# Theta's weights queued behind later softmax groups, and the rounding of x in theta's units on ScalarE for every batch

## The chip, the cores and the metric

The kernel runs on one core of a Trainium2 chip. TensorE (PE) multiplies matrices, its weight loads stand as PEld in the profile; VectorE (DVE), ScalarE (ACT) and GpSimd (POOL) work element by element; SyncE (SP) issues most DMAs. The metric is the device time of one execution in microseconds (us), as the median of several runs.

## The reference

Three parts follow one another on q, k, v of 4 batches, 8 heads, 576 positions and 64 values a head (model width 512). Attention keeps a window of 32 positions (first four heads) or 32 positions at a stride of 4 (the others):

```python
scores = np.where(masks, scale * q @ k.T, -1e9)
attn = exp(scores - max); attn = attn / (sum + 1e-9)
x = attn @ v                       # heads side by side: 576 x 512
theta = x @ w_theta
y = w_tok_r @ (x * cos(theta)) + w_tok_i @ (x * sin(theta))
u = x + y
x2 = u + np.maximum(u @ w_ch, 0)
h = np.maximum(x2 @ w_in, 0); u, v = h[:, :512], h[:, 512:]
v_n = (v - mean(v)) / sqrt(var(v) + 1e-6)
out = (u * (w_spatial @ v_n + b_spatial[:, None])) @ w_out
```

## The kernel before

Every product with a weight is made of three matmuls of float32r halves: high by high, high by low, low by high. A "rounding" makes the high half of a value (a copy to float32r), a subtraction the low half. Weights that come as 64 bit words are put together from bits first: `bits64` (L116 to L136) loads them (L123), scales them on POOL or ACT (L132, L130) and joins the bits with three DVE instructions (L133 to L135); `split_weight` (L138) then rounds (L108 on ACT, L110 on DVE, L112 on POOL) and subtracts (L146).

Attention of a batch has 12 groups of scores (`groups`, four pairs of heads by three groups). For each group PE makes the scores (L245 with the mask by matmul in batch 0, L252), DVE the maximum (L259 in batch 0; L263 and L264 elsewhere), ACT three exponentials with their sums (L267), DVE the sum's reciprocal (L268, L269), POOL the product `sm` (L270). Two groups later PE transposes it (L280) and DVE or ACT copies it (L282, `pT`); four groups later PE multiplies it with v (L294, L298), and ACT copies the result into x (L301, or L306, L307, L309, L310). Transposes and these results share three PSUM buffers (`ps_t`).

`th_unit` (L339) makes theta for 128 positions of a batch b: it rounds x in units of turns (`xh`, two buffers: ACT L352 for batch 0, DVE L354 for the others), takes the low half on DVE (`xl`, L355), does 12 matmuls (L360), removes whole turns (ACT L368, DVE L369), takes two sines on ACT (L377, L378), multiplies with x transposed (DVE L381; L388, L389 for the last rows) and splits the results zh and zl (L110, L112, L332). There are five units in batches 0 and 1, four in batch 2, one for the last 64 rows of batches 2 and 3 together (`xs`), and four in batch 3: 14 of the 19 are not of batch 0. `tm_run` (L415) multiplies with w_tok (L431, L438), `ch_run` (L446) with w_ch (L457). Batch b's token product runs among the attention of batch b+1.

Some weights are prepared in between and stored to DRAM for later: each part goes through one of two shared buffers `parts` (rounding, subtraction, then a store by SP, L159 for weights, L464 for x2 of a batch). Of w_spatial (`w_sp`, loaded into `stage` at L142) seven of eight parts are made among the attention of batch 3, the roundings on ACT (L108), the subtractions on POOL (L146). A part must wait for the store of the part two before it.

The order on each engine comes from a scheduler that works over the whole program with durations of its own (L841, `schedule_with_timeline_sim`), within the program's dependences. `behind` (L504) adds an edge without a semaphore: what is issued inside stands behind the given instruction on that instruction's engine. Theta's eight weight parts (`w_theta_job`, k and half c) are so tied to the exponentials, the reciprocal and the product of a group of the first softmax; nothing on SP is among these, so their DMAs are not tied. The three lines that set it:

```python
TH_FROM, TH_RATE = 6, 6
            if m == TH_FROM + TH_RATE * i // 10:
                behind(softmax[m], lambda: w_theta_job(i // 2, i % 2))
```

Parts 0 to 7 so stand behind groups 6, 6, 7, 7, 8, 9, 9 and 10 (counted from 0).

Of the kernel before, what the change touches and what calls it, by code (L numbers as in the profile page):

```python
# [16 lines left out]
ALU = mybir.AluOpType  # L17
# [19 lines left out]
INV2PI = float(np.float32(1.0 / (2.0 * math.pi)))  # L37
# [2 lines left out]


LAG_T, LAG_V = 2, 4
TH_FROM, TH_RATE = 6, 6
TOK_RATE = 2.25
ATT_RATE, ATT_RATE_PAIR = 2.0, 3.0
TAIL_RATE = 1.0
# [17 lines left out]
def tile_block(ctx: ExitStack, tc: tile.TileContext, qT, kT, vw, eye_in, mask_in, eye_b_in, w_theta, w_tok, w_ch, w_in, w_sp, w_sph, b_sp, w_out, out):  # L64
    nc = tc.nc
    V, A, G, PE, SY = nc.vector, nc.scalar, nc.gpsimd, nc.tensor, nc.sync

    def f32(ap):
        return ap.bitcast(F32)
# [260 lines left out]
    def split(dst_h, dst_l, src, eh="a", el="g"):  # L330
        copy(dst_h, src, eh)
        return (G if el == "g" else V).tensor_tensor(dst_l, src, f32(dst_h), op=ALU.subtract)  # L332

    def ztile(k, bufs=1):
        h = pz.tile([P, DM], F32R, tag=f"zh{k}", name=f"zh{k}", bufs=bufs)
        l = pz.tile([P, DM], F32R, tag=f"zl{k}", name=f"zl{k}", bufs=bufs)
        return h, l

    def th_unit(b, t, pair=False):  # L339


        n = P if pair or t < 4 else HALF
        if pair:
            src = xs[b]
            V.tensor_copy(src[:, :, HALF:], x[b + 1][:, :, 4 * P:])
        else:
            src = x[b][:, :, P * t:P * t + n]
        h = pth.tile([P, 4, P], F32R, tag="xh", name="xh", bufs=2)[:, :, :n]
        l = pth.tile([P, 4, P], F32R, tag="xl", name="xl", bufs=2)[:, :, :n]

        if b == 0:
            A.mul(h, src, INV2PI)  # L352
        else:
            V.tensor_scalar(h, src, INV2PI, None, op0=ALU.mult)  # L354
        V.scalar_tensor_tensor(l, src, INV2PI, f32(h), op0=ALU.mult, op1=ALU.subtract)  # L355
        ps = ps_mm.tile([P, 512], F32, tag="mm", name="ps_th")[:n]
        i = 0
        for k in range(4):
            for lh, rh in ((h, wth_h), (l, wth_h), (h, wth_l)):
                PE.matmul(ps, lh[:, k, :], rh[:, k, :], start=(i == 0), stop=(i == 11))  # L360
                i += 1
        if b == 0 and t in (0, 1):
            if not t:
                spare.append(p1.tile([P, 4, DM], F32, tag="uh", name="spare"))
            ta, tb = (spare[0][:, 2 * t + i, :] for i in range(2))
        else:
            ta, tb = (pth.tile([P, DM], F32, tag=g, name=g, bufs=2)[:n] for g in ("ta", "tb"))
        A.activation(ta, ps, AF.Identity, bias=magic[:n, 0:1])  # L368
        V.scalar_tensor_tensor(ta, ta, MAGIC, ps, op0=ALU.subtract, op1=ALU.subtract)  # L369
        xn = ps_t.tile([P, 512], F32, tag="pt", name="ps_xn")[:n]  # L370
        for k in range(4):
            turned[b, t] = PE.transpose(xn[:, P * k:P * (k + 1)], src[:, k, :], ident)
        if b == 0:
            A.activation(tb, ta, AF.Abs)
        else:
            V.tensor_scalar(tb.bitcast(U32), ta.bitcast(U32), 0x7FFFFFFF, None, op0=ALU.bitwise_and)
        A.activation(ta, ta, AF.Sin, scale=-TURN)  # L377
        ia = A.activation(tb, tb, AF.Sin, scale=-TURN, bias=half_pi[:n, 0:1])  # L378
        if t < 4:
            for k, tt in ((t, tb), (4 + t, ta)):  # L380
                iv = V.tensor_tensor(tt, xn, tt, op=ALU.mult)  # L381
                zh[b, k], zl[b, k] = ztile(k)
                zlast[b] = ia, iv, split(zh[b, k], zl[b, k], tt, Z_HI[k // 4], "g")
        else:
            for i in range(2 if pair else 1):
                r_ = slice(HALF * i, HALF * (i + 1))
                zz = pth.tile([P, DM], F32, tag=("ta", "tb")[i], name="zz", bufs=2)
                V.tensor_tensor(zz[:HALF], xn[r_], tb[r_], op=ALU.mult)  # L388
                V.tensor_tensor(zz[HALF:], xn[r_], ta[r_], op=ALU.mult)  # L389
                zh[b + i, 8], zl[b + i, 8] = ztile(8, 2)  # L390
                split(zh[b + i, 8], zl[b + i, 8], zz, "a", "g")
# [9 lines left out]
    def th_shared(b):  # L401
        th_unit(b, 4, True)
        yield

    def th_run(b, ts):
        for t in ts:
            th_unit(b, t)
            yield
# [436 lines left out]
```

## Time and profile before

| | us |
|---|---|
| median of 3 runs (554.42 to 559.04) | 554.44 |
| the profiled execution, its device time | 554.9 |
| its span, first to last instruction | 553.1 |
| PE busy | 531.0 |
| DVE busy | 320.3 |
| POOL busy | 262.9 |
| ACT busy | 244.2 |

Times in the trace are counted from the span's start. PE is the engine with the most work. A row of a timeline gives start, duration, engine, line, operation, and in brackets the idle time of the engine in front of it with what ended that. Idle time of another engine costs only what PE then waits.

### The profile page before, as it was taken

Reading aid. Unit: us, or ns where it says so; the run is one execution under the profiler, and the core shown is the slowest. Engines: PE = TensorE matmul, PEld = TensorE weight load, DVE = VectorE, ACT = ScalarE, POOL = GpSimd, SP = SyncE. Lnnn points to the kernel's source line nnn. Section 1 sums busy time; section 2 is a strip of 40 time slices with the busy share of each in tenths; the row PEclk is TensorE's granted clock in tenths of the full one; section 3 lists DMA queues with packets and bytes.
Section 4 is the critical chain, followed back from the end, with each engine's and each line's share of the span. In section 5 each row is a group of like instructions: output and inputs, shape, how many; then the busy total and the mean of one; then the engine's idle time right before and its main releaser. Section 6 shows DMA issues by size and latency. Waiting matters only on the chain.

```text
span 553.1 us, 11234 instructions
## 1 busy us (share of the span) xinstructions
PE 531.0 (96%) x4148; PEld 474.5 (86%) x4148; DVE 320.3 (58%) x835; ACT 244.2 (44%) x717; POOL 262.9 (48%) x333
## 2 busy tenths in 40 slices
PE   5997999999999999988999999999999999999997
PEld 3665888989889989877889999899899889988996
DVE  2698998898787487632694139862702148253020
ACT  3869765635656254663452114542322233233221
POOL 3494994645984359641188336363202204322040
PEclk9999999999999999998999999999999999999999
DMA  8925766660588353770005978848015110002002
GB/s 203 300 93 156 191 180 189 182 198 35 162 235 232 95 175 120 230 228 25 1 1 155 370 250 286 265 131 289 20 58 172 58 38 1 1 1 77 0 1 96
DMA packets 50223, 76.07 MB, mean 138 GB/s; under 512 B 4084, under 2 KB 30968, under 8 KB 50168
## 3 DMA queue, kind: packets, MB, share of 16 engines
q1 hardware_dynamic: 49944, 75.17, 44.3%
q8 instruction: 33, 0.54, 0.4%
q10 hardware_dynamic: 224, 0.18, 0.1%
q14 instruction: 22, 0.18, 0.1%
HBM read 52.53 MB, written 22.81 MB: 136 GB/s over the span
## 4 chain that ended last, share of the span: by engine, by line
PE 52%; DMA 3%; POOL 1%; ACT 1%; issue 1%; DVE 1%; SPq 0%; ACTq 0%; POOLq 0%; DVEq 0%
PE ps_sp L719 9%; PE ps_hu L700 9%; PE ps_o L748 9%; PE ps_hv L655 9%; PE ps_y L438 7%; PE ps_r L457 4%; PE ps_th L360 1%; DMA wsp_d<-parts 1%; DMA win_d<-parts 1%; PE ps_sp L722 1%; PE ps_sp L721 1%; POOL zl L332 0%; POOL parts L146 0%; ACT parts L108 0%; DVE ta L381 0%
## 5 line engine op out<-in xcount | busy, mean ns | idle before, releaser
L438 PE MATMUL ps_y<-wtok_h,zh 128*128 128x288 f32 x270 | 82.1, 308 | 0.7 <-DVE sm L263 0.4
L438 PE MATMUL ps_y<-wtok_h,zl 128*128 128x288 f32 x270 | 81.0, 301 | 0.4 <-POOL zl L332 0.4
L438 PE MATMUL ps_y<-wtok_l,zh 128*128 128x288 f32 x270 | 79.8, 299 | 0.0
L332 POOL TENSOR_TENSOR gl<-hu,gh 128x288 fp32r<-128x288 f32 x32 | 26.0, 813 | 71.4 <-ACT gh L108 71.4
L438 PEld LDWEIGHTS ps_y<-wtok_h,zh 128*128 128x128 f32 x270 | 50.7, 189 | 3.2 <-DVE sm L263 0.9
L438 PEld LDWEIGHTS ps_y<-wtok_h,zl 128*128 128x128 f32 x270 | 51.2, 189 | 1.7 <-POOL zl L332 0.8
L723 DVE TENSOR_TENSOR hu<-ps_sp,hu 128x288 f32<-128x288 f32 x32 | 14.6, 456 | 63.5 <-PE ps_sp L722 63.5
L438 PEld LDWEIGHTS ps_y<-wtok_l,zh 128*128 128x128 f32 x270 | 50.7, 189 | 0.6
L332 POOL TENSOR_TENSOR vl<-hv,vh 128x512 fp32r<-128x512 f32 x16 | 20.9, 1308 | 58.1 <-ACT vh L108 53.1
L270 POOL TENSOR_TENSOR sm<-sm,l 128x288 f32<-128x288 f32 x48 | 32.0, 672 | 27.6 <-DVE l L269 14.7
L267 ACT ACTIVATE sm<-sm,m 128x96 f32<-128x96 f32 x108 | 39.2, 364 | 12.8 <-DVE m L264 6.7
L332 POOL TENSOR_TENSOR ul<-x,uh 128x288 fp32r<-128x288 f32 x32 | 26.7, 841 | 26.4 <-ACT uh L108 26.1
L719 PE MATMUL ps_sp<-wsp_h,vh 128*128 128x288 f32 x128 | 37.8, 295 | 0.0
L457 PE MATMUL ps_r<-uh,wch_h 128*128 128x288 f32 x128 | 37.6, 300 | 0.2 <-DVE x L441 0.2
L719 PE MATMUL ps_sp<-wsp_l,vh 128*128 128x288 f32 x128 | 37.8, 295 | 0.0
L719 PE MATMUL ps_sp<-wsp_h,vl 128*128 128x288 f32 x128 | 37.8, 295 | 0.0
L700 PE MATMUL ps_hu<-x2h,win_h 128*128 128x288 f32 x128 | 37.7, 294 | 0.0
L700 PE MATMUL ps_hu<-x2h,win_l 128*128 128x288 f32 x128 | 37.7, 294 | 0.0
L700 PE MATMUL ps_hu<-x2l,win_h 128*128 128x288 f32 x128 | 37.7, 294 | 0.0
L457 PE MATMUL ps_r<-uh,wch_l 128*128 128x288 f32 x128 | 37.5, 296 | 0.0
L441 DVE TENSOR_TENSOR x<-ps_y,x 128x288 f32<-128x288 f32 x40 | 17.6, 448 | 33.9 <-PE ps_y L438 33.8
L457 PE MATMUL ps_r<-ul,wch_h 128*128 128x288 f32 x128 | 36.7, 295 | 0.0
(182 smaller groups left out, 1577.7 us busy)
## 6 DMA issues: line engine op xcount, KB each, us to landing
x2d<-parts SPq DMA_DIRECT2D x32, 288.0 KB, 2.7
vt<-vw SPq DMA_DIRECT2D x16, 432.0 KB, 4.6
w<-w_tok SPq DMA_DIRECT2D x18, 288.0 KB, 4.7
x2h<-x2d SPq DMA_DIRECT2D x8, 576.0 KB, 7.8
x2l<-x2d SPq DMA_DIRECT2D x8, 576.0 KB, 8.3
kt<-kT SPq DMA_DIRECT2D x15, 304.0 KB, 4.2
w<-w_in SPq DMA_DIRECT2D x16, 256.0 KB, 3.3
win_d<-parts SPq DMA_DIRECT2D x16, 256.0 KB, 2.5
```

Of the source, the lines that this page charges most:

```text
L267: ia = A.activation(sm[:, t, :], src[:, t, :], AF.Exp, bias=m_[:, t:t + 1], scale=scale, accum_out=l[:, t:t + 1])
L270: ig = G.tensor_tensor(sm, sm, l.unsqueeze(2).to_broadcast([P, 3, KW]), op=ALU.mult)
L332: return (G if el == "g" else V).tensor_tensor(dst_l, src, f32(dst_h), op=ALU.subtract)
L360: PE.matmul(ps, lh[:, k, :], rh[:, k, :], start=(i == 0), stop=(i == 11))
L438: PE.matmul(ps[:, :CH], lh[b, k][:, P * d:P * (d + 1)], rh[:, k, cs], start=(n == 0), stop=(n == 3 * len(ks) - 1))
L441: V.tensor_tensor(xv, ps[:, :CH], xv, op=ALU.add)
L457: PE.matmul(ps[:, :CH], lh[:, k, P * e:P * (e + 1)], rh[:, k, cs], start=(n == 0), stop=(n == 11))
L655: PE.matmul(ps, lh[:, k, ts_], rh[:, k, DM:], start=(n == 0), stop=(n == 11))
L700: PE.matmul(ps[:, :CH], lh[:, k, fs], rh[:, k, cs], start=(n == 0), stop=(n == 11))
L719: PE.matmul(ps[:, :CH], lh[b, k][:, fs], rh[:, k, cs], start=(n == 0), stop=False)
L723: V.tensor_tensor(t[:, f, cs], ps[:, :CH], t[:, f, cs], op=ALU.mult)
L748: PE.matmul(ps, lh[:, k, ts_], rh[:, k, cs], start=(n == 0), stop=(n == 11))
```

## The change

Theta's weight parts are tied to later groups: `TH_FROM + TH_RATE * i // 10` is now 8, 8, 9, 9, 10, 10, 11, 11. And `xh` is rounded on ACT in all 19 units. The new file has three lines fewer, so its line numbers from L355 on are lower by 3 (and ACT's rounding is L351 there).

```diff
-TH_FROM, TH_RATE = 6, 6
+TH_FROM, TH_RATE = 8, 5
...
-        if b == 0:
-            A.mul(h, src, INV2PI)
-        else:
-            V.tensor_scalar(h, src, INV2PI, None, op0=ALU.mult)
+        A.mul(h, src, INV2PI)
         V.scalar_tensor_tensor(l, src, INV2PI, f32(h), op0=ALU.mult, op1=ALU.subtract)
```

The first place is DVE in the first softmax, where theta's first weight part begins (`c64` and `w64g` are its bits, `m`, `l` and `pT` belong to attention). Before:

```order
L259 TENSOR_REDUCE m_468<-s_458 128x3
L133 TENSOR_SCALAR c64_96<-wth64_333 128x256
L282 COPY pT_311<-pt_307 96x384
L134 SCALAR_TENSOR_TENSOR c64_96<-w64g_335,c64_96 128x256
L268 TENSOR_SCALAR l_426<-l_426 128x3
L259 TENSOR_REDUCE m_512<-s_502 128x3
L135 SCALAR_TENSOR_TENSOR w64g_335<-w64g_335,c64_96 128x256
L269 RECIPROCAL l_426<-l_426 128x3
L133 TENSOR_SCALAR c64_96<-wth64_342 128x256
L259 TENSOR_REDUCE m_562<-s_552 128x3
```

And now:

```order
L259 TENSOR_REDUCE m_441<-s_431 128x3
L282 COPY pT_311<-pt_307 96x384
L268 TENSOR_SCALAR l_390<-l_390 128x3
L269 RECIPROCAL l_390<-l_390 128x3
L133 TENSOR_SCALAR c64_96<-wth64_399 128x256
L259 TENSOR_REDUCE m_485<-s_475 128x3
L259 TENSOR_REDUCE m_544<-s_534 128x3
L268 TENSOR_SCALAR l_442<-l_442 128x3
L134 SCALAR_TENSOR_TENSOR c64_96<-w64g_401,c64_96 128x256
L269 RECIPROCAL l_442<-l_442 128x3
```

The copy, a sum and its reciprocal now stand in front of the first weight part, and the maxima of the last two groups (m_512 and m_562 before, m_485 and m_544 now) close behind its first instruction.

The second place is SP in the attention of batch 3, with the parts of w_spatial (parts_3630, 3698, 3713, 3719, 3725, 3731 and 3992 are the first to the seventh, `vt` is v of a pair of heads). Before:

```order
L159 DMA wsp_d_75<-parts_3630 128x2x288
L218 DMA vt_3399<-vw 96x1152
L142 DMA stage_3726<-w_sp 128x288
L159 DMA wsp_d_75<-parts_3698 128x2x288
L142 DMA stage_3732<-w_sp 128x288
L159 DMA wsp_d_75<-parts_3713 128x2x288
L142 DMA stage_3993<-w_sp 128x288
L159 DMA wsp_d_75<-parts_3719 128x2x288
L218 DMA vt_3536<-vw 96x1152
L142 DMA stage_4224<-w_sp 128x288
L159 DMA wsp_d_75<-parts_3725 128x2x288
```

And now:

```order
L159 DMA wsp_d_75<-parts_3630 128x2x288
L142 DMA stage_3726<-w_sp 128x288
L159 DMA wsp_d_75<-parts_3698 128x2x288
L218 DMA vt_3399<-vw 96x1152
L142 DMA stage_3732<-w_sp 128x288
L159 DMA wsp_d_75<-parts_3713 128x2x288
L142 DMA stage_3993<-w_sp 128x288
L159 DMA wsp_d_75<-parts_3719 128x2x288
L142 DMA stage_4224<-w_sp 128x288
L159 DMA wsp_d_75<-parts_3725 128x2x288
L589 DMA stage_4533<-w_sph 128x288
L218 DMA vt_3536<-vw 96x1152
```

Each of the two loads of v has moved behind a store of parts: vt_3399 behind that of the second part, vt_3536 behind that of the fifth.

The third place is ACT in the same stretch, from the rounding of the fourth part on (sm_3545, sm_3569 and sm_3608 are the last three groups of batch 3). Before:

```order
L108 CAST parts_3719<-stage_3720 128x288
L301 COPY x3_3154<-ps_x_3443 128x384
L108 CAST parts_3725<-stage_3726 128x288
L282 COPY pT_3461<-pt_3457 96x384
L301 COPY x3_3154<-ps_x_3518 128x192
L282 COPY pT_3530<-pt_3526 96x384
L108 CAST parts_3731<-stage_3732 128x288
L267 ACTIVATE sm_3545,l_3547<-sm_3545,m_3546 128x96 x3
L267 ACTIVATE sm_3569,l_3571<-sm_3569,m_3570 128x96 x3
L108 CAST parts_3992<-stage_3993 128x288
```

And now:

```order
L108 CAST parts_3719<-stage_3720 128x288
L282 COPY pT_3423<-pt_3419 96x384
L267 ACTIVATE sm_3470,l_3472<-sm_3470,m_3471 128x96 x3
L108 CAST parts_3725<-stage_3726 128x288
L301 COPY x3_3154<-ps_x_3443 128x384
L282 COPY pT_3461<-pt_3457 96x384
L108 CAST parts_3731<-stage_3732 128x288
L301 COPY x3_3154<-ps_x_3518 128x192
L282 COPY pT_3530<-pt_3526 96x384
L108 CAST parts_3992<-stage_3993 128x288
L267 ACTIVATE sm_3545,l_3547<-sm_3545,m_3546 128x96 x3
L267 ACTIVATE sm_3569,l_3571<-sm_3569,m_3570 128x96 x3
```

The seventh part's rounding has moved in front of the exponentials of sm_3545 and sm_3569, and each of the others stands one group earlier.

## Rows read from the trace of the kernel before

**Rows 1.** The page: busy time, share of the span, instructions of PE.

```profile
PE 531.0 (96%) x4148; PEld 474.5 (86%) x4148; DVE 320.3 (58%) x835; ACT 244.2 (44%) x717; POOL 262.9 (48%) x333
```

**Rows 2.** One stretch of 10 us: length, busy PE, PEld, DVE, ACT, POOL, then clock, DMA, GB/s.

```profile
50.00:60.00 10.00, 8.16 (x56) 6.39 (x55) 9.97 (x20) 8.22 (x17) 8.77 (x9) 1.00 0.94 246
```

**Rows 3.** Timeline of DVE, first softmax and theta of batch 0.

```profile
23.90 0.43 DVE L133 TENSOR_SCALAR c<-wth 128x256 uint32<-128x256 uint32 x1 [1.68 <-DMA wth<-w_theta]
24.24 0.54 DVE L282 COPY pT<-pt 96x384 f32<-96x384 f32 x1
...
25.34 0.44 DVE L259 TENSOR_REDUCE m<-s 128x3 f32<-128x288 f32 x1
...
47.95 0.68 DVE L388 TENSOR_TENSOR zz<-ps_xn,tb 64x512 f32<-64x512 f32 x1 [1.26 <-ACT tb L378]
```

**Rows 4.** Timeline of POOL, the same stretch.

```profile
23.96 0.42 POOL L132 TENSOR_SCALAR w64g<-wth 128x256 f32<-128x256 f32 x1 [2.66 <-DMA wth<-w_theta]
24.34 0.67 POOL L270 TENSOR_TENSOR sm<-sm,l 128x288 f32<-128x288 f32 x1
...
39.41 0.74 POOL L146 TENSOR_TENSOR wth_l<-w64g,wth_h 128x256 fp32r<-128x256 f32 x1
```

**Rows 5.** Timeline of PE: a wait in the first attention, theta's first and last shared matmuls.

```profile
27.78 0.87 PE L280 MATMUL pt<-ident,sm 128*96 128x128 f32 x6 [1.07 <-ACT x L301]
...
35.47 0.47 PE L360 MATMUL ps_th<-wth_h,xh 128*64 128x512 f32 x1
...
40.90 0.62 PE L360 MATMUL ps_th<-wth_l,xh 128*64 128x512 f32 x2
```

**Rows 6.** The lines of the rounding of x: instructions, duration min/median/max in ns.

```profile
L352 ACT ACTIVATE xh<-x x5: 420/617/627, 34.8 to 50.2; 128x512 fp32r<-128x512 f32 x4, 128x256 fp32r<-128x256 f32 x1
...
L354 DVE TENSOR_SCALAR xh<-x x13: 414/428/958, 110.7 to 275.5; 128x512 fp32r<-128x512 f32 x12, 128x256 fp32r<-128x256 f32 x1
```

**Rows 7.** Timeline of ACT, batch 2's theta and batch 3's attention.

```profile
194.01 0.43 ACT L108 CAST parts<-x 128x288 fp32r<-128x288 f32 x1 [2.93 <-DMA win_d<-parts]
...
245.25 0.43 ACT L108 CAST parts<-stage 128x288 fp32r<-128x288 f32 x1 [1.59 <-DMA wsp_d<-parts]
245.59 0.37 ACT L267 ACTIVATE sm<-sm,m 128x96 f32<-128x96 f32 x1
...
249.58 0.43 ACT L108 CAST parts<-stage 128x288 fp32r<-128x288 f32 x1 [1.73 <-issue]
...
250.54 0.36 ACT L267 ACTIVATE sm<-sm,m 128x96 f32<-128x96 f32 x1
```

**Rows 8.** Timeline of SP's queue, batch 3's attention.

```profile
242.43 0.38 SPq L159 DMA_DIRECT2D wsp_d<-parts  x1
242.90 0.42 SPq L218 DMA_DIRECT2D vt<-vw  x1
...
244.04 0.38 SPq L159 DMA_DIRECT2D wsp_d<-parts  x1
```

**Rows 9.** Timeline of POOL, batch 3's attention, its last product.

```profile
252.28 0.67 POOL L270 TENSOR_TENSOR sm<-sm,l 128x288 f32<-128x288 f32 x1 [0.77 <-DVE l L269]
```

**Rows 10.** Timeline of PE, its three longest waits in batch 3's attention.

```profile
242.06 0.50 PE L280 MATMUL pt<-ident,sm 128*96 128x128 f32 x3 [1.69 <-ACT x L301]
...
251.57 0.53 PE L280 MATMUL pt<-ident,sm 128*96 128x128 f32 x3 [1.83 <-POOL sm L270]
253.00 0.53 PE L280 MATMUL pt<-ident,sm 128*96 128x128 f32 x3 [0.90 <-POOL sm L270]
```

**Rows 11.** The same view by single microseconds, end of batch 3's attention.

```profile
250.00:251.00 1.00, 0.00 (x0) 0.00 (x0) 0.07 (x1) 1.00 (x6) 0.92 (x2) 1.00 0.02 6
...
252.00:253.00 1.00, 0.10 (x1) 0.00 (x0) 0.46 (x2) 0.79 (x4) 0.67 (x1) 1.00 0.69 242
...
254.00:255.00 1.00, 1.00 (x16) 0.88 (x13) 0.00 (x0) 0.47 (x2) 0.00 (x0) 0.54 0.00 0
...
257.00:258.00 1.00, 1.00 (x15) 0.88 (x12) 0.00 (x0) 0.36 (x2) 0.00 (x0) 0.76 0.00 0
```

## The prediction

> **What bounds the kernel now.** I read the page first, for the engine with the most work. PE is busy 531.0 of a span of 553.1 us [rows 1], so all its waits together are 22.1 us, and nothing that this change touches makes or removes a matmul. What can be won or lost is therefore a part of those waits, and one thing besides, the granted clock. I then listed PE's waits in order of time. They lie in four places: the start of the program, which the change leaves alone, the first attention with theta of batch 0, from 24 to 54 us, the middle of the attention of batch 3, from 240 to 254 us, and half a microsecond here and there. From 75 to 215 us PE is full. The reader is to see in the timeline of PE which instruction ended each wait: an x copy of ACT in the first attention (1.07 us) [rows 5], and then in batch 3 another x copy (1.69 us) and twice the product `sm` of POOL (1.83 and 0.90 us) [rows 10]. Last I looked at the clock by single microseconds: behind that second pair of waits, in which PE was busy 0.00 of one microsecond and 0.10 of another, the granted clock stood at 0.54 in the microsecond from 254 and was back only within that from 257, where it was 0.76 [rows 11]. That is about 3.4 us at the lower of the two levels (1.2 instead of 2.4 GHz), in which PE did the work of half that time, so 1.7 us were lost there.
>
> **Part A, theta's weights in the first softmax.** Before, DVE comes to theta's first weight part at 23.90 − 1.68 = 22.22 us and stands 1.68 us until its DMA has landed, at 23.90 [rows 3]; POOL stands 2.66 us for the same DMA [rows 4]. Attention's work is queued behind on both: on DVE the copy `pT`, the sum's step L268 and the maximum of the next group, on POOL a product `sm`. With the edges moved to groups 8 to 11 the copy, the sum and the reciprocal pass in front of the weight part, while DVE would have idled, and `sm` of groups 8 and 9 passes on POOL. Between the first weight instruction (starting 23.90) and the maximum at 25.34 there stood three others from 24.24 on; they are gone from there, so the maximum starts about 24.24, that is 25.34 − 24.24 = 1.10 us earlier [rows 3]. The last groups follow from it, and theta's first matmul, at 35.47, can start by as much earlier [rows 5].
>
> What is late next? First, the weights themselves: eight parts now stand behind later groups, and the last low half was made on POOL at 39.41 + 0.74 = 40.15, while the last matmuls of the first unit's chain that need it started at 40.90 [rows 4, 5]. The margin of 0.75 us stays if the weights gain as much as the attention, which they do in my replay of the order, since they are the same instructions without the waits between them. Second, DVE. From 50 to 60 us it is busy 9.97 of 10 us [rows 2], with w_tok's bits, the multiplications with cosine and sine, and their halves, and the amount of that work is the same. A gain ahead reaches the end of this stretch only if DVE does not idle more in it. Before, DVE idled 1.26 us ahead of 47.95 for a sine of ACT [rows 3]; in the changed order two of w_tok's bit instructions (L134, L135; about 0.43 us each by the row of L133) have been put behind those products, so that the wait grows by 0.87. Of 1.10 us then 1.10 − 0.87 = 0.2 are left. These are the bounds, −0.2 and −1.1 us; I take the middle, −0.6, because the order between shifts in more places than I could follow by hand.
>
> **Part B, the rounding of x.** It concerns 14 of the 19 units. The rounding took 617 ns on ACT and 428 on DVE at the median [rows 6], so ACT gets 14 × 0.617 = 8.6 us more and DVE 14 × 0.428 = 6.0 us less (some of DVE's took up to 958 ns, so up to 7). ACT is busy 244.2 us and DVE 320.3 of the span [rows 1]; both have room. In batches 1 and 2 these units run while PE has token and channel matmuls queued, and PE waits for nothing there, so I cost it at 0. The cover is these matmuls. Without it each unit's chain is longer by 0.617 − 0.428 = 0.19 us, in all 14 × 0.19 = 2.7 us. The other bound: DVE's 6.0 us are no gain where PE does not wait, except in the half microsecond here and there, so −0.5. One thing is new: `xh` now stands on ACT behind roundings of `parts`, which can wait long for a store (2.93 us at 194.01) [rows 7]. Two buffers of `xh` are ahead of PE by one unit of matmuls, which I count as enough.
>
> Here the trace shows 617 against 428 ns for the same tile. The Trainium skill ("ScalarE: Activation LUTs", Rules for kernel authors) says that a multiplication belongs on VectorE and not on ScalarE, up to about three times faster per element in bf16; the rows here, in float32, agree in direction at a ratio of 1.44. By the rule the change would cost the 2.7 us above; by the full PE in those stretches it costs nothing.
>
> DVE's own rounding spread from 414 to 958 ns [rows 6], so something held some of them. The Trainium skill ("SBUF — State Buffer", Who interferes with whom) says that DVE and GpSimd share one pair of ports, held exclusively. By that, POOL would gain too from roundings that leave DVE, an estimate of at most the same 6.0 us of its 262.9; as PE does not wait for POOL in those units, the sum would be the same.
>
> **Part D, the attention of batch 3.** Nothing in the diff names it, but its order changes most. The parts of w_spatial run through two shared buffers. A rounding on ACT must wait for the store of the part two before. These stores are short when nothing is in front of them: that issued at 242.43 let ACT go on at 245.25, so 2.82 us later. That issued at 244.04, just behind a load of v (242.90), let ACT begin the seventh rounding at 249.58 only, 5.54 us later [rows 7, 8]. Both loads of v are now behind the stores (the second place of the change). If the store then takes 2.82 us, the seventh rounding can start at 244.04 + 2.82 = 246.86, 2.7 us earlier.
>
> But ACT's order changes too (the third place). The six exponentials of sm_3545 and sm_3569 stood in front of the seventh rounding, from 245.59 on, each 0.37 us with no gap, 6 × 0.36 = 2.15 us. They now stand behind it. From the first exponential of the last group (250.54) to its product on POOL (252.28) there were 1.74 us [rows 7, 9]. If the seventh rounding starts at 246.86 and holds ACT for 0.34 (as from 245.25 to 245.59), then six exponentials (2.15), the two x copies that stood between the seventh rounding and the last three exponentials (250.54 − 249.58 − 0.34 = 0.62), and 1.74 to the last product make 246.86 + 0.34 + 2.15 + 0.62 + 1.74 = 251.7, so 0.6 us earlier than 252.28. If the fifth and the sixth rounding, too, come earlier by the same shift of a load (the third store, that behind the first load of v), up to 1.7 us more: 2.4 us earlier. If the store is not shortened, the last product is 2.15 us later. Bounds −2.4 and +2.15. I take −1.6, in the upper half of the gain, because the exponentials of these groups are ready before the rounding is, and because both loads have left the places in front of the stores. PE's two waits there, 1.83 + 0.90, allow a gain of that size.
>
> The clock is taken as it is: PE still waits in this place, and what it then does at 0.5 costs 1.7 us as before. Bounds −1.7 (the clock stays up) and +1.7 (twice as long at the low level).
>
> **Sum.** A −0.6, B 0, D −1.6: −2.2 us. On the profiled execution, which took 554.9, that is 552.7; it lies 0.5 above the median of 554.44, so the median becomes 552.2.
>
> **Rivals.**
> 1. *The seventh rounding stands in front of the exponentials, and its store is not shortened.* Then a wait takes the place of the one removed, and the time is longer. The load of v is still close by in the queue, all transfers run together, and DMA is the cause if it is the amount in flight rather than the order that makes 5.54 us. Price: +2.15 for the exponentials, +1.7 for a second stretch at the low clock, −0.6 from A: 554.4 + 3.3 = 557.7. It decides at 249.58 − 2.15 = 247.43: a seventh rounding that starts later than that makes batch 3 slower. If the rounding before it slips likewise, 2.7 more, 560.4. Against it: the store without a load in front took half as long.
> 2. *Nothing comes through.* DVE's full stretch eats A, since its work is the same, or the weights are late by more than the 0.75 us of margin, so that PE waits for `wth_l` in place of the last attention group; in D gains and losses meet. 554.4, ±0.6. For it: 9.97 of 10 us [rows 2].
> 3. *The rounding on ACT is on the path after all*: +2.7 on the forecast, 554.9. Against it: PE is full there.
> 4. *The waits in batch 3 go altogether*, all three (1.69 + 1.83 + 0.90 = 4.42) [rows 10], with them the low clock (1.7), and A gives its full 1.1: 554.4 − 7.2 = 547.2. For it: the clock is lost only behind long waits. Against it: the chain of stores stays, only in another order.
>
> **How the numbers follow.** The forecast (a gain of 0.6 to 4 us) 0.42; rival 1 0.20; rival 2 0.20; rival 3 0.05; rival 4 0.13. A measurement of this kernel can tell about 1% from no change, that is 5.5 us. Slower by over 1% needs rival 1 with a second slip, 0.07 of its 0.20. Faster by over 1% needs most of rival 4: 0.10 of its 0.13. The rest, 0.83, is within 1%. The range runs to 549.0 below (the forecast with D −2.4, A −1.1 and the clock −1.7 is 549.2) and to 557.8 above (rival 1 at its own price); outside lie 0.10 and 0.07. The forecast's own range, for it holds less than half, is 550.4 to 553.8.
>
> **What would show it right or wrong.** Right: theta's first matmul at about 34.4 us; the first matmul of batch 1's channel product a few tenths earlier; the seventh rounding at about 247, with a store of about 2.8 us ahead of it, and PE's last two waits in batch 3 together near 1 us in place of 2.73; `xh` on ACT at 0.62 us without a wait of PE for it. Wrong: a seventh rounding behind 247.4, or a new wait of PE for `wth_l` or `xh`, or a second stretch of granted clock below 1 (each a loss); or no stretch below 1 at all, which is rival 4.

## The result: 0.8% slower, outside the range

The changed kernel took 561.15 us as the median of 15 executions, the kernel before 555.51 of 15 beside it. One execution of the changed kernel (566.98 us) fell into a slower state of the chip and is left out of the ratio, which is 1.0082 with a 95% interval of 1.0061 to 1.0103; that is 4.6 us slower (3.4 to 5.7). The forecast was 552.2 with a range up to 557.8. The difference is under the 1% that the prediction took for the least that can be told, but the interval does not reach 1, the sign is the other one, and the range did not hold the time.

The profiled execution took 560.36 us with a span of 558.6, against 554.9 and 553.1. The page of the changed kernel answers to [rows 1]:

```profile
PE 534.4 (96%) x4148; PEld 476.9 (85%) x4148; DVE 323.4 (58%) x818; ACT 252.9 (45%) x734; POOL 264.8 (47%) x333
```

PE's busy time rose by 3.4 us with the same matmuls, and its waits by 5.5 − 3.4 = 2.1 us, from 22.1 to 24.2. The first is the granted clock. DVE is the odd one: 14 roundings left it, 6.6 + 0.4 us in the trace before, and with them three copies `pT` (1.6 us), and it is busier by 3.1 us.

PE's timeline in the changed kernel, theta's first matmul and those instructions ahead of which it waited longest:

```profile
33.50 0.47 PE L357 MATMUL ps_th<-wth_h,xh 128*64 128x512 f32 x1
53.31 0.79 PE L357 MATMUL ps_th<-wth_h,xl 128*128 128x512 f32 x1 [2.54 <-DVE xl L352]
...
124.51 0.50 PE L357 MATMUL ps_th<-wth_h,xl 128*128 128x512 f32 x1 [0.62 <-DVE xl L352]
172.49 0.53 PE L280 MATMUL pt<-ident,sm 128*96 128x128 f32 x3 [1.43 <-POOL sm L270]
...
229.39 1.23 PE L252 MATMUL s<-kt,qz 128*64 128x96 f32 x12 [2.62 <-DVE sm L263]
250.23 0.50 PE L280 MATMUL pt<-ident,sm 128*96 128x128 f32 x3 [1.41 <-ACT x L301]
258.28 1.16 PE L280 MATMUL pt<-ident,sm 128*96 128x128 f32 x6 [0.36 <-POOL sm L270]
290.99 0.40 PE L435 MATMUL ps_y<-wtok_h,zh 128*128 128x288 f32 x1 [1.57 <-DVE x L438]
```

The waits of [rows 10], 4.42 us, have become 1.41 + 0.36 = 1.77. In their place stand waits that the kernel before had not, or had shorter: 2.54 at 53 us (0.80 before), 0.62 and 1.43 in the stretch in which PE had been full, 2.62 at 229, 1.57 at 291 (0.32 before). The granted clock, by stretches (length, PE, PEld, DVE, ACT, POOL busy, clock, DMA share, GB/s):

```profile
51.00:52.00 1.00, 0.00 (x0) 0.00 (x0) 1.00 (x2) 0.97 (x2) 1.00 (x2) 0.71 0.00 0
54.00:55.00 1.00, 1.00 (x4) 0.81 (x3) 0.90 (x3) 0.63 (x1) 1.00 (x2) 0.50 0.42 58
58.00:59.00 1.00, 1.00 (x7) 0.90 (x7) 0.92 (x2) 0.54 (x1) 1.00 (x2) 0.87 0.88 295
...
228.00:230.00 2.00, 0.61 (x8) 0.61 (x10) 1.97 (x8) 0.54 (x5) 2.00 (x4) 0.73 0.09 31
230.00:232.00 2.00, 2.00 (x14) 1.78 (x12) 1.03 (x3) 1.94 (x11) 1.42 (x3) 0.50 0.09 15
```

Each of the two long waits has a stretch at the lower level (0.50) with it, of about 7 us, most of it behind the wait; the stretch of [rows 11] is gone. In a single profile this looks like most of the loss. Over the timed executions it isn't: the clock of one and the same kernel varies from one execution to the next (the kernel before: 0.982 to 1.000 as the mean of an execution, at 552.0 to 560.3 us), and its mean over them was 0.9909 before (in the executions beside the experiments) and 0.9895 after, which is an estimated 0.0014 × 558 = 0.8 us of the 4.6 (with an error of some 1 us). The profiled execution of the kernel before, at 0.997, was one of those that lost little.

### The profile page after: what moved, and what is told of

Same layout as the page of the kernel before. It is cut to its first block, busy times and chain, and to the rows that moved or that the text cites. A ratio compares the mean times of both kernels' runs of the same rounds, so it can differ in the third digit from the quotient of the medians.

```text
span 558.6 us, 11251 instructions
## 1 busy us (share of the span) xinstructions
PE 534.4 (96%) x4148; PEld 476.9 (85%) x4148; DVE 323.4 (58%) x818; ACT 252.9 (45%) x734; POOL 264.8 (47%) x333
## 4 chain that ended last, share of the span: by engine, by line
PE 72%; DVE 9%; DMA 5%; issue 4%; ACT 4%; POOL 4%; SPq 1%; ACTq 0%; POOLq 0%; DVEq 0%
PE ps_y L435 14%; PE ps_sp L716 9%; PE ps_hu L697 9%; PE ps_o L745 9%; PE ps_hv L652 9%; PE ps_r L454 7%; PE s L252 4%; PE ps_th L357 3%; DMA win_d<-parts 2%; PE pt L280 2%; DMA wsp_d<-parts 1%; PE ps_x L294 1%; DVE xl L352 1%; PE ps_y L428 1%; POOL parts L146 1%
## 5 line engine op out<-in xcount | busy, mean ns | idle before, releaser
L108 ACT CAST gh<-hu 128x288 fp32r<-128x288 f32 x32 | 13.8, 433 | 52.7 <-DVE hu L720 52.7
```

## The experiments

All ratios are to the kernel before on the same chip.

| run | ratio | 95% interval |
|---|---|---|
| the change | 1.0082 | 1.0061 to 1.0103 |
| e1, edges alone | 0.9977 | 0.9942 to 1.0012 |
| e2, rounding alone | 1.0088 | 1.0058 to 1.0117 |
| e3, change, PE's wait filled | 1.0039 | 1.0012 to 1.0066 |
| e4, change, batch 2 on DVE | 1.0052 | 1.0021 to 1.0082 |
| e5, change, batches 2 and 3 on DVE | 1.0028 | 1.0002 to 1.0055 |
| e10, change, batch 1 on DVE | 1.0030 | 1.0010 to 1.0049 |
| e6, change, three xh everywhere | 1.0100 | 1.0065 to 1.0136 |
| e7, change, a third xh in batches 1 to 3 | 1.0045 | 1.0018 to 1.0071 |
| e8, change, tb of batch 2 on ScalarE | 1.0006 | 0.9975 to 1.0036 |
| e9, edges alone, one zh on ScalarE | 0.9944 | 0.9922 to 0.9967 |
| e11, before, one zh on ScalarE | 1.0040 | 1.0015 to 1.0066 |
| e12, change, zh and all tb on ScalarE | 1.0022 | 0.9996 to 1.0049 |

**The two edits apart.** That they can be told apart is a property of this schedule: with the edges alone PE's order differs from that of the kernel before only up to the first transposes of batch 1's attention, and with the rounding alone only from batch 1's theta to that of batch 3. A good marker between is the run of 24 matmuls of ps_x that started at 107.66 us before and at 108.61 after.

e1:

```diff
-TH_FROM, TH_RATE = 6, 6
+TH_FROM, TH_RATE = 8, 5
```

> Only the edges of theta's weights are moved (8, 5); x is rounded as before. Theory 1 (each edit loses in a place of its own: the edges bring the attention ahead, but the first theta units then run into POOL's burst of zl, DVE's zh and xl get 1.35 and 1.75 us instead of 0.42 and 1.10, PE waits about 2.5 us near 51 to 53 us and the granted clock falls to 0.5 for some 7 us): the 24 matmuls of ps_x that stood at 107.66 us in the kernel before and at 108.61 in the changed one stand at about 108.6, and the whole is 1 us slower than before (0 to +2). Rival (the edges only gain, the loss is all the rounding's): 1.5 to 2 us faster than before. Rival (the edges alone cause all of it): 4.6 us slower.

e2:

```diff
-        if b == 0:
-            A.mul(h, src, INV2PI)
-        else:
-            V.tensor_scalar(h, src, INV2PI, None, op0=ALU.mult)
+        A.mul(h, src, INV2PI)
```

> Only the rounding of x is on ScalarE for every batch; theta's weights are tied to groups 6 to 10 as before. Theory 1: up to 110 us as before; then PE waits about 2.6 us in the attention of batch 3 (for DVE's masked scores) and falls to the lower clock for 3 to 4 us, and waits 1 to 1.6 us near 290; 3.5 to 4.6 us slower than before. Rival (the rounding is hidden, as the prediction costed it): within 0.7 us of before. Rival (a full sum: 14 times 0.19 on the path): 2.7 us slower without a new wait of more than 0.5 us.

The rounding alone costs the whole loss, and the edges cost nothing that can be told: −1.3 us (−3.2 to +0.7) against +4.9 (3.2 to 6.5). The mean clock of e2's executions was 0.9872 against 0.9912, so an estimated 0.004 × 556 = 2.2 us of its loss came with the clock (error 1.7); e1's was as before. PE's timeline of e1, and under it of e2:

```profile
54.13 0.50 PE L360 MATMUL ps_th<-wth_h,xl 128*128 128x512 f32 x1 [2.55 <-DVE xl L355]
...
109.45 0.92 PE L294 MATMUL ps_x<-pT,vt 96*64 96x64 f32 x24
```

```profile
227.53 1.23 PE L252 MATMUL s<-kt,qz 128*64 128x96 f32 x12 [2.61 <-DVE sm L263]
...
289.93 0.40 PE L435 MATMUL ps_y<-wtok_h,zh 128*128 128x288 f32 x1 [2.05 <-DVE x L438]
```

The places came out as theory 1 had them: 2.55 us at 54 with the edges, with the marker late (109.45), and 2.61 near 228 and 2.05 near 290 with the rounding. Its sum for the edges (1 us slower) did not: what they lose at the front is made up later, so that the span is 553.1 as before. In the profile it is made up in batch 3, where the waits of [rows 10] are 0.94 + 0.93 + 0.94 us in e1, in the same order of instructions as before. The marker is a coarse measure: it stood between 108.61 and 112.94 in the seven profiles with the edges moved and the same order up to it (the change, e1, e4, e5, e7, e8, e10), and at 107.66 and 108.22 in the two with the edges of before.

**The clock at 51 to 59 us.** e3 adds five matmuls of zeros (ten instructions in its trace) to an accumulation, behind the two matmuls of ps_y ahead of the wait; the edit, shortened:

```diff
 PE.matmul(accs[e][:, :CH], lh[b, k][:, P * e:P * (e + 1)], rh[:, k, cs], ...)
+for _ in range(5 if i + j == 0 and e else 0):
+    PE.matmul(accs[e][:, :CH], x[0][D:, 0, :P], qzero[0][D:, 0, :CH], start=False, stop=False)
```

> The changed kernel with five matmuls more on PE, of zeros added to an accumulation, put where PE waits for xl in the theta of batch 0 (51 to 53 us); the result is not altered by them. If the fall of the granted clock there comes from that wait, the clock stays at 1.00 from 50 to 60 us, theta's matmuls behind it take 0.39 instead of 0.63 us each, and the 24 matmuls of ps_x stand at about 106 to 106.5 instead of 108.61. If the clock falls for another reason, it is at 0.5 there as before and the matmuls stand at 108.6 or later. The whole time is less telling, since the order behind shifts: 2 us faster than the changed kernel by the first, the same or slower by the second.

The stretches of e3, and two instructions of its PE's timeline:

```profile
52.00:54.00 2.00, 2.00 (x9) 1.35 (x8) 2.00 (x3) 0.94 (x2) 2.00 (x2) 1.00 0.00 0
54.00:56.00 2.00, 2.00 (x11) 1.64 (x10) 1.90 (x5) 1.25 (x3) 1.50 (x3) 1.00 0.55 142
56.00:58.00 2.00, 2.00 (x17) 1.95 (x16) 2.00 (x5) 2.00 (x5) 1.64 (x3) 1.00 0.92 295
...
226.00:228.00 2.00, 0.00 (x0) 0.00 (x0) 1.97 (x5) 1.12 (x6) 2.00 (x3) 1.00 0.37 120
228.00:230.00 2.00, 1.95 (x22) 1.83 (x23) 1.97 (x7) 1.37 (x7) 2.00 (x4) 1.00 0.03 8
```

```profile
50.90 2.69 PE L431 MATMUL ps_y<-qz,x 64*128 64x288 f32 x10
...
59.41 0.35 PE L253 MATMUL s<-kt,qz 128*64 128x96 f32 x2 [1.00 <-DVE ta L379]
```

Half of the expectation held. With PE busy in the wait the clock stays at 1.00. In each of the seven profiles that have this wait (2.54 or 2.55 us) it fell to 0.50, inside the wait or at most 1.2 us behind its end, so that the wait brings the fall there is well supported. It doesn't always: near 228 PE waited 2.61 us in e3 as well, and the clock stayed at 1.00, while it fell for some 3 us at 42 us, behind waits of 1.14 and 0.59. The other half did not hold: the marker stands at 108.90, not at 106 to 106.5. PE then waits for DVE (1.00 us at 59.41) and for a load of q (1.01 us at 65.59). From 50 to 60 us DVE is busy 9.9 of 10 us, and a faster PE only finds it sooner. The run's time was 0.4% better than the change's; its order also differs further on, so that isn't put down to the clock alone.

**Where the rounding costs.** Three runs put it back on DVE for some of the batches, by a condition in front of `A.mul`:

```diff
-        A.mul(h, src, INV2PI)
+        if b == 2 and not pair:          # e4;  e5: b >= 2;  e10: b == 1
+            V.tensor_scalar(h, src, INV2PI, None, op0=ALU.mult)
+        else:
+            A.mul(h, src, INV2PI)
```

> The changed kernel, but in the four units of batch 2 x is rounded on DVE again (9 or 10 of the 14 units stay on ScalarE). PE's order is the changed kernel's up to the theta of batch 2 and again from the attention of batch 3 on. Theory 2 (the loss of the rounding sits in batch 2's theta: xh waits in ScalarE's order behind ta and the sines of the unit before, xl and tb behind it, so that zh and zl are some 4 us late when the attention of batch 3 is spread over them): PE's wait of 2.6 us near 228 us is at most 0.6 us, the granted clock stays at 1.00 from 215 to 240, and the whole is 4 to 5 us faster than the changed kernel, so 0 to 1 us off the kernel before; the wait of 1.6 to 2 us near 290 stays. Rival (ScalarE's 8.6 us more delay the attention of batch 3 itself, or the loss is spread evenly): 1 to 1.5 us faster than the changed kernel, and the wait near 228 stays over 2 us.

> The changed kernel with x rounded on DVE in the units of batches 2 and 3 (only batch 1's five move to ScalarE). Theory 2: as the run before, and the wait near 290 us is 0.5 us instead of 1.6 to 2; 1 to 2 us faster than that run, 1 to 3 us faster than the kernel before. Rival (the unit of batch 1 are the costly ones): no faster than the run before.

> The changed kernel, but in the five units of batch 1 x is rounded on DVE again. Theory (each batch's theta pays a share, batch 1 too, by the difference of the timed runs 2.9 us): PE's waits near 124 us (0.5 to 0.6) and 172 us (1.4) are gone, and the whole is 1 to 3 us faster than the changed kernel, 0.3 to 0.6% slower than before. Rival (all of the loss is in batches 2 and 3): as the changed kernel, 0.8% slower than before.

PE in e4, and in e10:

```profile
220.07 0.40 PE L438 MATMUL ps_y<-wtok_h,zl 128*128 128x288 f32 x1 [0.39 <-POOL zl L332]
221.15 0.40 PE L438 MATMUL ps_y<-wtok_h,zh 128*128 128x288 f32 x1 [0.54 <-DVE sm L263]
...
285.30 0.40 PE L438 MATMUL ps_y<-wtok_h,zh 128*128 128x288 f32 x1 [1.59 <-DVE x L441]
```

```profile
227.28 1.23 PE L252 MATMUL s<-kt,qz 128*64 128x96 f32 x12 [2.61 <-DVE sm L263]
```

Each wait belongs to the batch whose rounding was moved. With batch 2 on DVE the wait of 2.62 is 0.39 + 0.54 and the clock is 1.00 from 215 to 240; the wait near 290 stays at 1.59 and goes to 0.32 with batch 3 on DVE. With batch 1 on DVE PE has no wait from 75 to 215 us, and the one at 227 stays. The times share the loss out differently from theory 2, which had put it all in batch 2 and had e5 faster than the kernel before (it is 0.28% slower): from the edges (−0.23%) batch 1 adds 0.51, batch 3 0.24, batch 2 0.30, and taken from the other end batch 1 is 0.82 − 0.30 = 0.52. Each of these has an error of 0.3 to 0.45. So no batch pays the whole alone, and only batch 1's share is clear of zero. In e5's profile no wait of PE from 75 to 215 us is over 0.6 us, so where batch 1's share arises is not shown.

**What holds it up.** In batch 2's theta the changed kernel's ScalarE waits for DVE. (`ta` is what is left of theta without whole turns, `tb` its absolute value, which the cosine needs.) ScalarE, and under it DVE:

```profile
205.29 0.67 ACT L365 ACTIVATE ta<-ps_th,magic 128x512 f32<-128x512 f32 x1
205.86 0.62 ACT L351 ACTIVATE xh<-x 128x512 fp32r<-128x512 f32 x1
206.38 0.42 ACT L108 CAST parts<-x 128x288 fp32r<-128x288 f32 x1
211.20 0.63 ACT L374 ACTIVATE ta<-ta 128x512 f32<-128x512 f32 x1 [4.40 <-DVE tb L373]
```

```profile
207.76 0.84 DVE L110 CAST zh<-tb 128x512 fp32r<-128x512 f32 x1
208.52 1.21 DVE L352 SCALAR_TENSOR_TENSOR xl<-x,xh 128x512 fp32r<-128x512 f32 x1
209.66 1.51 DVE L373 TENSOR_SCALAR tb<-ta 128x512 uint32<-128x512 uint32 x1
```

The last xh stands on ScalarE (205.86) behind ta of the unit two before (205.29); DVE has put its xl (208.52) in front of that earlier unit's tb (209.66), and the earlier unit's sines on ScalarE wait 4.40 us for tb. DVE in turn waits 0.95 us for those sines at 212.48, but not for xh in this place: xh was ready, and DVE worked without a pause. Its zh, xl and tb took 0.84 + 1.21 + 1.51 = 3.56 us here, where the shortest of each are 0.42, 0.68 and 0.41, so some 2 us of the 4.40 are the stretching that is looked at below. Before, xh and xl followed each other on DVE at 200.38 and 201.38 and needed nothing from ScalarE. Two runs give xh a third buffer, so that it can be rounded ahead of its turn, everywhere (e6) or only for the third unit of batches 1 to 3 (e7); a third takes DVE's step tb out of the ring (e8):

```diff
-h = pth.tile([P, 4, P], F32R, tag="xh", name="xh", bufs=2)
+h = pth.tile([P, 4, P], F32R, tag="xh", name="xh", bufs=3)                  # e6
+h = pth.tile([P, 4, P], F32R, tag=("xh", "xhx")[b > 0 and t == 2], name="xh", bufs=(2, 1)[b > 0 and t == 2])   # e7
...
-        if b == 0:
+        if b in (0, 2) and not pair:                                        # e8
             A.activation(tb, ta, AF.Abs)
```

> The changed kernel with three buffers of xh instead of two; all roundings on ScalarE. Theory 2 in its narrow form (the late xh of batch 2 is a matter of the buffer: a third lets ScalarE round before ta and the sines): the wait near 228 us falls below 1 us, and the whole is 2 to 4 us faster than the changed kernel. Rival (the buffer is not what holds it, but ScalarE's order and the DVE and POOL instructions that collide behind it): the wait stays above 2 us and the time within 1 us of the changed kernel.

> The changed kernel with a third buffer of xh that only the third unit of batches 1, 2 and 3 uses, so that the first 100 us stay as in the changed kernel (the run with three buffers everywhere shifted them). Theory 3 (a ring of two engines: xh waits in ScalarE's order for the sines before it, these for tb of DVE, tb stands behind xl on DVE, xl waits for xh; a buffer more lets xh of the third unit go in front): the wait near 228 us is below 1 us, the granted clock there 1.00, and the whole 1.5 to 3.5 us faster than the changed kernel (0.2 to 0.6% slower than the kernel before on the same chip). Rival (the buffer plays no part, ScalarE's added time is what counts): the wait stays over 2 us, 0.8% slower than before.

> The changed kernel, and in the four units of batch 2 the absolute value tb is made on ScalarE as in batch 0, not on DVE. This puts 4 times 0.6 us more on ScalarE, but takes the step through DVE out of the ring. Theory 3: ScalarE's wait of 4.4 us for tb (in the run with the rounding alone, at 209 us) is gone, PE's wait near 228 us is below 1.3 us, 0.5 to 2.5 us faster than the changed kernel. Rival (ScalarE simply has too much work there): the wait near 228 grows to 3 us or more, 0.5 to 2 us slower than the changed kernel.

PE and ScalarE in e8:

```profile
224.67 0.40 PE L435 MATMUL ps_y<-wtok_h,zh 128*128 128x288 f32 x1 [0.38 <-DVE sm L263]
```

```profile
210.61 0.63 ACT L371 ACTIVATE tb<-ta 128x512 f32<-128x512 f32 x1 [0.86 <-DVE ta L366]
```

e8 is the telling one: ScalarE got still more work, and its wait of 4.40 fell to 0.86, PE's of 2.62 to 0.38, and the time to that of the kernel before (1.0006). So what held PE there was the way through DVE's queue, not the amount of ScalarE's work. e8 also takes four instructions of 0.81 to 1.51 us off DVE, so by itself it doesn't tell the order of the queues from DVE's load; e7 does for the wait, since it leaves these four on DVE. e8's gain, 0.76%, is more than theory 3 had and more than that of e4 (0.30), which took the same wait away; the intervals overlap, and the difference is left open. In e6 and e7 the wait near 228 is gone too (in its place 0.38, 0.41, 0.56 and 0.53 between 215 and 227 us in e7). e7 gained 0.37%. e6 gained nothing: its first 100 us came out in another order, with waits of 2.14 us for DVE's `spare` at 53 and 2.93 for a load of q at 59, which is what e7 was made to avoid.

**What stretches DVE's instructions.** In the first theta, where the edges lose, two instructions of DVE took far longer than in the kernel before. DVE and POOL of the changed kernel:

```profile
49.63 0.68 DVE L366 SCALAR_TENSOR_TENSOR spare<-spare,ps_th 128x512 f32<-128x512 f32 x1
50.23 1.35 DVE L110 CAST zh<-spare 128x512 fp32r<-128x512 f32 x1
51.50 1.75 DVE L352 SCALAR_TENSOR_TENSOR xl<-x,xh 128x512 fp32r<-128x512 f32 x1
```

```profile
50.03 1.27 POOL L332 TENSOR_TENSOR zl<-zz,zh 128x512 fp32r<-128x512 f32 x1
51.26 3.14 POOL L332 TENSOR_TENSOR zl<-spare,zh 128x512 fp32r<-128x512 f32 x2
```

The same two of the kernel before, and POOL's beside them:

```profile
51.94 0.42 DVE L110 CAST zh<-spare 128x512 fp32r<-128x512 f32 x1
52.27 1.10 DVE L355 SCALAR_TENSOR_TENSOR xl<-x,xh 128x512 fp32r<-128x512 f32 x1
```

```profile
52.00 0.84 POOL L112 TENSOR_SCALAR zh<-spare 128x512 fp32r<-128x512 f32 x1
52.80 1.73 POOL L332 TENSOR_TENSOR zl<-zz,zh 128x512 fp32r<-128x512 f32 x1
```

Before, the rounding started 0.06 us ahead of POOL's instruction, took 0.42, and POOL's got longer. After, POOL's zl was 0.20 us ahead, and the rounding ended 0.28 us behind it, after 1.35. Together DVE's two took 1.58 us more, and PE's wait grew by 1.74. An operand in PSUM seems to protect: `ta` (L366) took 0.67 to 0.69 wherever it stands here. e9 takes this one rounding off DVE, on top of the edges; e11 does so in the kernel before:

```diff
-split(zh[b, k], zl[b, k], tt, Z_HI[k // 4], "g")
+split(zh[b, k], zl[b, k], tt, "a" if b == 0 and k == 0 else Z_HI[k // 4], "g")
```

> The edges alone (x rounded as before), and in batch 0 one rounding, that of the first zh of unit 0, is on ScalarE instead of DVE: it is the one that took 1.35 us on DVE while POOL made zl. Theory (DVE held up by POOL in this place sets PE's wait for xl near 53 us): the wait of 2.55 us falls to 1.0 to 1.6 us, the matmuls of ps_x stand 0.5 to 1.2 us earlier than with the edges alone, and the whole is 0.3 to 0.6% faster than the kernel before. Rival (only the rounding's own 0.42 us count): the wait falls to 2.1 to 2.2 us and the time is that of the edges alone. A second way to fail: xl takes over the collision and gets longer by as much.

> The kernel before (edges 6 to 10, x rounded as before), with the first zh of unit 0 in batch 0 on ScalarE. In the kernel before this rounding took 0.42 us on DVE. Theory (the edges bring 1.5 to 2 us, which the collision took away again, and the 0.56% of the run with both came from both together): this edit alone gives 0.5 us or less, within 0.2% of the kernel before. Rival (the gain was this edit's alone, whatever the edges): 0.4 to 0.6% faster than before.

In e9, DVE and, under it, PE; last PE in e11:

```profile
51.31 1.61 DVE L355 SCALAR_TENSOR_TENSOR xl<-x,xh 128x512 fp32r<-128x512 f32 x1
```

```profile
52.98 0.80 PE L360 MATMUL ps_th<-wth_h,xl 128*128 128x512 f32 x1 [1.13 <-DVE xl L355]
...
108.09 0.92 PE L294 MATMUL ps_x<-pT,vt 96*64 96x64 f32 x24
```

```profile
62.74 0.61 PE L431 MATMUL ps_y<-wtok_h,zl 128*128 128x288 f32 x1 [1.68 <-POOL zl L332]
```

The wait fell from 2.55 to 1.13 us and the marker came 109.45 − 108.09 = 1.36 us earlier, a little more than expected; it is also ahead of the seven profiles without this edit, by 0.52 us or more. xl alone still runs into POOL (1.61). e9 is 0.56% faster than the kernel before (0.33 to 0.78), the only one of the runs that beats both kernels beyond its interval. That gain isn't to be seen at the marker, where its profile is 0.43 us behind that of the kernel before. Its executions had a mean clock of 0.9951 against 0.9906, by the same estimate 0.0045 × 554 = 2.5 us of 3.1 (error 1.3), so most of the gain seems to have come with the clock; what kept the clock up is not shown. The same edit without the edges (e11) is 0.40% slower, worse than either side had: PE there no longer waits for xl, but 1.68 us for zl. So the gain is not this rounding's alone, whatever the edges.

**Both mended.** e12 is the changed kernel with e9's edit and |ta| on ScalarE in all units (`if b >= 0`).

> The changed kernel (edges moved, all roundings of x on ScalarE) with two mends: the first zh of unit 0 in batch 0 on ScalarE, and the absolute value tb on ScalarE in all units, so that no unit's sines wait for DVE's queue. Theory 3 (the rounding costs by the ring, not by its work on ScalarE): PE's waits near 53, 124, 172 and 228 us are each below 1.3 us, and the whole is 0.2 to 0.6% faster than the kernel before, although ScalarE has some 17 us more work. Rival (ScalarE's work counts in batches 1 and 3): 0.3% or more slower than before.

PE in e12:

```profile
51.84 0.50 PE L357 MATMUL ps_th<-wth_h,xl 128*128 128x512 f32 x1 [1.14 <-DVE xl L352]
...
123.26 0.50 PE L357 MATMUL ps_th<-wth_h,xl 128*128 128x512 f32 x1 [0.63 <-DVE xl L352]
...
220.43 0.40 PE L435 MATMUL ps_y<-wtok_h,zh 128*128 128x288 f32 x1 [0.37 <-DVE sm L263]
```

All four waits are below 1.3 us as expected (near 172 us there is none over 0.3), and the time is 0.6% below the change's, but it is not faster than the kernel before (1.0022, 0.9996 to 1.0049), and 0.8% behind e9, which has the roundings on DVE; its executions even had the higher clock (0.9962 against 0.9925 before). Without the two mends the roundings cost 1.05% (the change against e1), so with them a good part of the price is still there. e8 alone would put most of it on the ring, e4 and e12 would not: how much is the ring's, and how much ScalarE's added work and the new order, stays open.

## Why the prediction was wrong, step by step

**Part B is the step that failed.** It priced the rounding on ScalarE at 0, because PE is full in batches 1 and 2, and its upper bound at 2.7 us as 14 times the difference of the two durations. Measured alone it is 4.9 us, above that bound. Three things were missing. The step asked whether PE waits now, not what DVE still has to do when the next stage begins: the last zh of batch 2's theta was made on DVE at 225.31 us where it had been 217.31, among the attention of batch 3, and PE's waits show up there and behind it, for DVE's masked scores at 229 (2.62) and for its x at 291 (1.57), in stretches that the step did not look at. It argued with batches 1 and 2 alone, though five of the 14 units belong to batch 3, one of them shared with batch 2, and the wait near 290 went with their roundings (e5). And it added up durations, where the order matters: xh on ScalarE stands behind another unit's `ta`, and xl on DVE in front of that unit's `tb`. That this order makes the wait at 229 is shown by e7, which changes nothing but a buffer and what the scheduler makes of it; that it makes the whole loss is not shown. The prediction did name the queue (`xh` behind a waiting rounding of `parts`) and set it aside with two buffers of xh; in e7 a third buffer took the wait near 228 away.

**The relief of DVE did not come.** 6 to 7 us were to leave DVE. Its busy time rose by 3.1 us instead, because its other instructions took longer. The rows by line, before and after, with minimum, median and maximum in ns:

```profile
L376 DVE TENSOR_SCALAR tb<-ta x14: 407/426/1002, 122.1 to 289.1; 128x512 uint32<-128x512 uint32 x13, 64x512 uint32<-64x512 uint32 x1
```

```profile
L373 DVE TENSOR_SCALAR tb<-ta x14: 410/788/1514, 124.4 to 295.0; 128x512 uint32<-128x512 uint32 x13, 64x512 uint32<-64x512 uint32 x1
```

The median of tb went from 426 to 788 ns, and ScalarE's waits for it from 11.3 to 16.4 us in all. Of these 28 instructions five took over 0.6 us before and nine after, and at the start of each POOL had an instruction under way that ran on for 0.33 to 1.23 us; of the 14 short ones this holds for one. The prediction had the rule for this and read half of it. The Trainium skill ("SBUF — State Buffer", Who interferes with whom) says that, where a DVE instruction contends with GpSimd for the shared ports, whichever of the two issues first holds them for its whole instruction and the other blocks. The trace agrees, 0.42 against 1.35 us for one rounding, by which of the two was ahead. The prediction took from it that POOL would gain, and not that a shift of half a microsecond can turn the collision round. POOL did not gain either: 262.9 us became 264.8.

**Part A was right in its mechanism and wrong in what was late next.** Attention did come forward, by about the 1.10 forecast or more: theta's first matmul moved from 35.47 to 33.50, and to 34.53 in e1, which has the same order there. The weights were not late. But the gain was to be 0.6 us net, and at the marker the kernel was 0.95 late. The step named the full DVE of [rows 2] as what would eat the gain, and the wait behind the sines did grow (1.26 to 1.50), but the larger part was the collision with POOL, which the step did not have: e9, which takes one of the two collided instructions away, has 1.36 us of it back.

**Part D was right, in mechanism and size.** The seventh rounding followed its store by 2.49 us (250.61 to 253.10) where it had been 5.54:

```profile
250.61 0.38 SPq L159 DMA_DIRECT2D wsp_d<-parts  x1
...
251.59 0.40 SPq L218 DMA_DIRECT2D vt<-vw  x1
```

```profile
253.10 0.43 ACT L108 CAST parts<-stage 128x288 fp32r<-128x288 f32 x1 [1.63 <-DMA wsp_d<-parts]
```

PE's last two waits there became one of 0.36, where near 1 was forecast, and no low clock followed. In these two profiles the gain is 4.42 − 1.77 = 2.65 us against the 1.6 taken, in a stage that was some 8 us late by then (250.23 against 242.06). But 4.42 is the highest of five profiles with the order of before in this stage (e1 2.81, e5 2.85, e9 3.03, e11 3.83), and those with the new one have 1.77, 1.47 (e2) and 2.09 (e10): 3.4 against 1.8 in the mean, so the 1.6 was met. The intervals from store to rounding are farther apart, 4.76 to 5.54 against 2.45 to 2.49 us. Since e2 has this gain and e1 has not, it is the rounding's, and the 4.9 us are what was left after it.

Rival 1 did not happen. Rival 3 (the rounding on the path) was the true one with 0.05, and its size was a mere sum; no rival had it above 2.7. The clock, taken as it is with bounds of 1.7 us, lost more than that in the profile, by the two stretches of about 7 us, but only some 0.8 us over the executions. Two readings were off without weight: PE had a wait of 1.20 us at 70.28, outside the four places, and D's bound of 2.4 is 0.6 + 1.7 = 2.3, with no row for the 1.7.

## What to carry to other kernels

When an operation moves to another engine, list what stands in front of it in that engine's queue and what waits for it in the queue it left: if the two lists name each other's results, the price can be a round trip each time, and the difference of the two durations is no bound for it. That the engine with the most work is full at a place says nothing on work that it will want later; ask by how much that work is ahead. And two elementwise engines that hold each other up, as DVE and POOL do here, can change places by half a microsecond and turn a hidden collision into one on the path (0.42 against 1.35 us), so durations are best read as a minimum and a maximum, with the neighbour's row beside the maximum.

## What was not expected of the hardware

The mean granted clock of a whole execution varied between 0.982 and 1.000 for one and the same kernel, and its time, loosely with it, by 8 us; in a kernel that waits often, one profile's low stretches say little of the next execution's. With one wait filled with matmuls the clock was 1.00 in that place (e3), yet the place behind it came no earlier, since DVE set its pace; and a wait of 2.61 us later in the same profile left the clock at 1.00 too, where the same wait in three others (the change, e2, e10) had a stretch of 0.50 with it. And DVE gained busy time by giving work away: 323.4 against 320.3 us.
